# A second bank for h and a second pair for y after the attention, and the low parts of k on VectorE

## The chip, the cores and the metric

The kernel runs on one core of a Trainium2 chip. The metric is the device time of one execution in microseconds (us). The core has five engines, each with a queue of its own that it works through in order: TensorE (PE; its weight loads are a row of their own, PEld), VectorE (DVE), ScalarE (ACT), GpSimd (POOL) and SyncE (SP), which here issues nearly all DMAs. Engines wait for each other by semaphores. Matmuls write to PSUM, which has eight banks of 2 KB per partition; everything else lies in SBUF or DRAM.

## The reference

Three layers, one after the other, all in float32 outside the chip:

```
attn_out: q, k, v of shape (4, 8, 576, 64)
scores = q @ k.T / sqrt(64); scores under (row maximum - tau) are masked out
attn   = exp(scores - max) / (sum + 1e-9);  attn_out = attn @ v
x = attn_out as (2304, 512)
h = x @ w_in (512 x 2048);  g = h * sigmoid(h);  y = g @ w_out (2048 x 512)
a = y @ w_a; b = y @ w_b (512 x 1536 each);  out = (a * b) @ w_o2 (1536 x 512)
```

## The kernel before

**Attention.** A pair of heads of one batch is worked on together. It has nine tiles of 128 query rows against 576 keys, 144 tiles in all. PE writes the scores of a tile to `sa` (two PSUM banks, one buffer; the first 16 tiles also use `sb`); DVE takes the row minimum of the negated scores and moves them to `t` (`L489`), which frees `sa`; ACT takes the exponential (`L503`); DVE masks by the threshold and sums (`L506`); PE turns the masked tile by transposes into `tp` (`L538`, two banks), ACT copies it out, PE multiplies with v (`L583`, bank `av`). The sums are inverted, sent through DRAM (`r_d`, read back as `xi`) and multiplied on by POOL (`L618`); the result goes to DRAM as `xT_d`.

From tile 54 on, heads come in by `split_head`: ACT copies q and k to rounded high parts in the tile `sp` (`L399`), and two POOL instructions, both released by that copy, subtract these to get the low parts: `L405` for q (64 partitions) and `L402` for k (128 partitions, 576 columns). PE then needs two matmuls instead of one slower one (`L473`).

**First MLP.** Nine tiles of 256 tokens by 16 blocks of 128 hidden columns make 144 units, numbered n; a tile j has units 16j to 16j + 15. Weights and activations are each held as a high and a low part. A unit's up-projection is 12 matmuls of 256 columns into the one bank `hb` (`L699`); then ACT takes tanh (`L708`), DVE multiplies the gate out of tanh and h (`L711`), which frees `hb`, ACT rounds it to gh (`L714`) and DVE subtracts for gl (`L717`). The down-projection is 12 more matmuls (`L746`), eight with gh and four with gl, that add to the four outputs of the tile, in the pair of banks `sb`. PE's order is up-projection of unit n, down-projection of unit n - 1, and so on. After a tile's last unit, ACT halves one bank of `sb` (`L763`) and DVE the other (`L765`), which frees the pair, and the result goes to DRAM as `yT_d`. PE works on these units between the attention's instructions and alone after them.

**Second MLP.** Four tiles of 512 tokens and one of 256, by 12 blocks, make 60 units: `ps_a` and `ps_b` (12 matmuls each, `L825`), a copy, a product, high and low part, and 12 matmuls down (`L869`). After the attention its inputs (`yr`, split by `L799` and `L802`) and its weights are made ready: 36 pieces of 512 columns, each some eight instructions on ACT, DVE and POOL (`L312` to `L340`, tiles `wraw`, `wt`, `wc`, `w`).

**PSUM.** During the attention the banks are `sb` 2, `hb` 1, `sa` 2, `tp` 2, `av` 1. After it, `close_attention` gives the last five to `ps_a` and `ps_b`, two each, with one left over. After the first MLP, `close_mlp1` gives `sb` and `hb` to the outputs of the second.

**The order.** Nothing is ordered by hand. `Plan` collects tasks, each with an engine, an estimated cost (`act_ns`, `dve_ns`, `pool_ns`, `pe_ns`), a rank, the tasks it waits for, and the rings (buffers) it takes; it then plays time forward and gives each free engine its ready task of lowest rank. What comes out is the order of each engine's queue in the built program. DVE and POOL are assumed to share a port: a task marked `port` is made longer by what it overlaps with the other engine, at most by its own cost. `closed` and `closed1` are tasks without an instruction, at which pools are closed and opened.

Of the kernel before, what the change touches and what calls it, by code (L numbers as in the profile page):

```python
# [52 lines left out]

WARM = 9

FILL = 0.6
# [148 lines left out]
def fused_kernel(ctx: ExitStack, tc: tile.TileContext, qk, qk2, v, tau, w_in, w_out, w_a, w_b, w_o2, out):  # L205
# [19 lines left out]
    def pool(stack, name, bufs, side="left", **kw):  # L225
# [4 lines left out]
    p1, att = ExitStack(), ExitStack()  # L230
    RINGS = dict(qk=2, sp=2, v=1, t=2, e=4, pa=1, pb=1, sa=1, sb=1, tp=2, hb=1, av=1, x=1, xi=1, rs=1,
                 xr=2, xb=8, g=2, th=1, yo=2, wraw=2, wc=1, wt=2, w=32, w2=4,
# [157 lines left out]
    def split_head(n, b, h):  # L390
        s = {"split": True}

        def load():
            s["r"] = ap["qk"].tile([P, 2 * S], F32, name="qk")
            nc.sync.dma_start(out=s["r"], in_=qk2[b, h])

        def hi():
            s["t"] = pools["sp"].tile([P, 3, S], F32R, name="sp")
            nc.scalar.copy(out=s["t"][:, :2], in_=s["r"].rearrange("p (a s) -> p a s", a=2))  # L399

        def lo_k():
            nc.gpsimd.tensor_tensor(out=s["t"][:, 2], in0=s["r"][:, S:], in1=s["t"][:, 1].bitcast(F32), op=ALU.subtract)  # L402

        def lo_q():
            nc.gpsimd.tensor_tensor(out=s["t"][D:, 0], in0=s["r"][D:, :S], in1=s["t"][D:, 0].bitcast(F32), op=ALU.subtract)  # L405

        ld = dma(n + R_LD, P * 8 * S, load, take=["qk"])
        up = add("ACT", act_ns(2 * S), n + R_SPLIT, hi, [ld], ["sp"], behind=closed0)
        q, k = (add("Pool", pool_ns(S), n + R_SPLIT, f, [up]) for f in (lo_q, lo_k))
        att_tasks.append(ld)  # L410
        pl.free("qk", q, k)
        s["ready"] = [q, k]
        return s
# [273 lines left out]
    def mlp1_up(n, j, f):  # L687

        s = gs[j, f] = {}

        def up(c):
            def fn():
                if c == 0:
                    s["h"] = ps_1.tile([P, 512], F32, name="hb")[:, :TB]
                w = wt["in", c, f // 4]
                o = (f % 4) * P
                x = xs[j]
                for k, (a, xx) in enumerate(((1, x["h", c]), (0, x["h", c]), (0, x["l", c]))):
                    nc.tensor.matmul(s["h"], lhsT=w[:, a, o:o + P], rhs=xx,  # L699
                                     start=(c == 0 and k == 0), stop=(c == NC - 1 and k == 2))  # L700
            return fn
# [18 lines left out]
        for c in range(NC):  # L720
            p = pl.add("PE", 3 * pe_ns(TB), R, up(c),
                       [*x_ready[j, c], *w_ready["in", c, f // 4]], ["hb"] if c == 0 else [], behind=[up_last[0]])
            up_last[0] = p
            w_last["in", c, f // 4] = p
            if f == NF - 1:
                pl.free("xb", p)
        th = pl.add("ACT", act_ns(TB, True), R_AUX, tanh, [p], ["g", "th"])
        ga = pl.add("DVE", dve_ns(TB), R_AUX, gate, [th])
        pl.free("hb", ga)
        hh = pl.add("ACT", act_ns(TB), R_AUX, hi, [ga])  # L730
# [4 lines left out]
    def mlp1_down(n, j, f):  # L735

        prods = [(e, a, "gh") for e in range(NC) for a in (1, 0)] + [(e, 0, "gl") for e in range(NC)]

        def down(k0):
            def fn():  # L740
                if f == 0 and k0 == 0:
                    ys[j] = ps_1.tile([P, 2, 512], F32, name="sb").rearrange("p k (e t) -> p (k e) t", e=2)
                w = wt["out", f]
# [8 lines left out]
        for k0 in (0, 4, 8):  # L752
            p = pl.add("PE", 4 * pe_ns(TB), R, down(k0), [g_ready[j, f][k0 == 8], *w_ready["out", f]],
                       ["sb"] if f == 0 and k0 == 0 else [], behind=[down_last[0]])
            down_last[0] = p
        w_last["out", f] = p
        pl.free("g", p)
        if f == NF - 1:
# [14 lines left out]
            for k in range(2):  # L773
# [4 lines left out]
                y_dma.append(st)  # L778
            pl.free("sb", *evs)

# [32 lines left out]
    def mlp2_up(n, t0, f):  # L813
# [3 lines left out]
        def up(nm, c):  # L817
            def fn():
                if c == 0:
                    s[nm] = pools["ab"].tile([P, T2], F32, name=f"ps_{nm}")  # L820
                w = wt[nm, c, f // 4]
# [22 lines left out]
        for nm in "ab":  # L844
            for c in range(NC):
                p = pl.add("PE", 3 * pe_ns(tn), 1e5 + 2 * n, up(nm, c), [*y2_ready[t0, c], *w_ready[nm, c, f // 4]],
                           ["z" + nm] if c == 0 else [], behind=[up_last[0]])
                up_last[0] = p
# [56 lines left out]
    for b in range(1, B):  # L905
        for c in range(NC):
            pair(b, c, (0, 1))
    units = [(j, f) for j in range(NB) for f in range(NF)]
    for n, u in enumerate(units):
# [11 lines left out]

    def close_attention():
        att.close()
        right.close()
        open_transit()
        pools["w2"] = pool(ctx, "wpool2", RINGS["w2"], "right")
        pools["y"] = pool(ctx, "yb", 6, "right")
        pools["ab"] = pool(ctx, "ps_ab", 2, "right", space=PSUM)

    def close_mlp1():  # L930
        p1.close()
        pools["z"] = pool(ctx, "z", 2)
        pools["ob"] = pool(ctx, "o", 2)
        pools["o_ps"] = pool(ctx, "ps_o", 1, space=PSUM)

    closed = pl.add("none", 1, 0, close_attention, behind=[*att_tasks, *closed0])
    closed1 = pl.add("none", 1, 0, close_mlp1, behind=[up_last[0], down_last[0], closed, *y_dma])
# [58 lines left out]
```

## Time and profile before

| | |
|---|---|
| time, median of 3 runs | 1202.97 us (1200.87 to 1204.55) |
| profiled execution, its own time | 1202.49 us |
| its span | 1200.7 us |
| PE busy | 1162.6 us (97%) |
| DVE busy | 648.1 us (54%) |
| ACT busy | 544.5 us (45%) |
| POOL busy | 278.9 us (23%) |
| mean granted clock of PE | 0.995 |

The profile is of one execution, whose time is the span and the little that lies around it. The granted clock is a share of TensorE's full 2.4 GHz; the other level is 1.2 GHz, 0.50. The shares of busy time are means over stages that differ: the attention (to about 491 us) loads all engines, the first MLP's remaining units (to about 752 us) mostly PE, and the second MLP PE alone. So they are read stage by stage below. In a timeline row, `[1.46 <-DVE th L711]` means that the engine sat idle for 1.46 us ahead of this instruction, and that what ended it was a DVE instruction of line 711 that wrote or read `th`.

### The profile page before, as it was taken

Reading aid. Unit: us, or ns where it says so; the run is one execution under the profiler, and the core shown is the slowest. Engines: PE = TensorE matmul, PEld = TensorE weight load, DVE = VectorE, ACT = ScalarE, POOL = GpSimd, SP = SyncE. Lnnn points to the kernel's source line nnn. Section 1 sums busy time; section 2 is a strip of 40 time slices with the busy share of each in tenths; the row PEclk is TensorE's granted clock in tenths of the full one; section 3 lists DMA queues with packets and bytes.
Section 4 is the critical chain, followed back from the end, with each engine's and each line's share of the span. In section 5 each row is a group of like instructions: output and inputs, shape, how many; then the busy total and the mean of one; then the engine's idle time right before and its main releaser. Section 6 shows DMA issues by size and latency. Waiting matters only on the chain.

```text
span 1200.7 us, 19670 instructions
## 1 busy us (share of the span) xinstructions
PE 1162.6 (97%) x7675; PEld 998.2 (83%) x7675; DVE 648.1 (54%) x1428; ACT 544.5 (45%) x1071; POOL 278.9 (23%) x232
## 2 busy tenths in 40 slices
PE   8889989999999999989999999999999999999998
PEld 5556667888888888889999999888888888888898
DVE  7989898777777777473233258765311211221121
ACT  7777777666666666443233245443211211211121
POOL 3656554233322322130000024443000000000000
PEclk9989999999999999999999999999999999999999
DMA  5655543222322220351010023432200200000000
GB/s 190 195 176 150 160 152 129 80 85 86 97 72 71 89 89 32 101 166 36 1 37 27 1 66 117 152 123 71 70 1 1 70 1 1 18 36 1 1 36 18
DMA packets 43276, 90.14 MB, mean 75 GB/s; under 512 B 4384, under 2 KB 22448, under 8 KB 43184
## 3 DMA queue, kind: packets, MB, share of 16 engines
q1 hardware_dynamic: 43040, 88.89, 23.0%
q8 instruction: 60, 0.98, 0.4%
q14 instruction: 32, 0.26, 0.1%
q10 hardware_dynamic: 144, 0.00, 0.0%
HBM read 74.65 MB, written 14.23 MB: 74 GB/s over the span
## 4 chain that ended last, share of the span: by engine, by line
PE 76%; DVE 10%; DMA 5%; issue 4%; ACT 4%; POOL 1%; SPq 0%; DVEq 0%; ACTq 0%; POOLq 0%
PE op L869 12%; PE ps_b L825 12%; PE ps_a L825 12%; PE hb L699 12%; PE sb L746 12%; PE av L583 5%; PE tp L538 5%; PE sa L473 4%; DVE e L506 3%; DMA xi<-r_d 2%; DVE t L489 1%; DVE wraw L323 1%; DVE thr L497 1%; DVE wc L328 1%; DVE gl L717 1%
## 5 line engine op out<-in xcount | busy, mean ns | idle before, releaser
L699 PE MATMUL hb<-xh,w 128*128 128x256 f32 x1152 | 225.1, 290 | 6.0 <-DVE th L711 3.9
L699 PEld LDWEIGHTS hb<-xh,w 128*128 128x128 f32 x1152 | 179.3, 192 | 14.2 <-DVE th L711 6.2
L746 PE MATMUL sb<-gh,w 128*128 128x256 f32 x1152 | 169.6, 286 | 2.3 <-DVE yo L765 1.8
L699 PE MATMUL hb<-xl,w 128*128 128x256 f32 x576 | 162.9, 283 | 0.0
L835 DVE TENSOR_TENSOR z<-ps_b,z 128x512 f32<-128x512 f32 (+1 forms) x60 | 38.2, 636 | 230.2 <-PE ps_b L825 230.2
L746 PEld LDWEIGHTS sb<-gh,w 128*128 128x128 f32 x1152 | 150.5, 192 | 6.6 <-DVE yo L765 2.8
L506 DVE SCALAR_TENSOR_TENSOR e<-t,thr,e 128x576 f32<-128x576 f32 x128 | 129.7, 1014 | 21.8 <-ACT e L503 20.8
L825 PE MATMUL ps_a<-yh,w 128*128 128x512 f32 (+1 forms) x480 | 137.0, 370 | 0.0
L825 PE MATMUL ps_b<-yh,w 128*128 128x512 f32 (+1 forms) x480 | 136.6, 369 | 0.0
L869 PE MATMUL op<-w,zh 128*128 128x512 f32 x432 | 134.3, 392 | 0.0
L489 DVE TENSOR_SCALAR_CACHE_REDUCE t<-sa,nscale 128x576 f32<-128x576 f32 x128 | 103.6, 809 | 51.6 <-PE sa L473 49.6
L538 PE MATMUL tp<-ident,e 128*128 128x128 f32 x706 | 106.5, 280 | 13.9 <-DVE e L506 10.0
L711 DVE SCALAR_TENSOR_TENSOR th<-th,hb 128x256 f32<-128x256 f32 x144 | 60.2, 418 | 107.2 <-ACT th L708 106.8
L332 POOL TENSOR_TENSOR wt<-wc,wt 128x512 uint32<-128x512 uint32 x68 | 91.2, 1342 | 109.5 <-DVE wc L328 91.3
L503 ACT ACTIVATE e<-t,min 128x576 f32<-128x576 f32 x128 | 99.6, 780 | 28.2 <-DVE t L489 27.5
L708 ACT ACTIVATE th<-hb 128x256 f32<-128x256 f32 x144 | 55.0, 382 | 122.3 <-PE hb L699 113.2
L699 PEld LDWEIGHTS hb<-xl,w 128*128 128x128 f32 x576 | 110.1, 191 | 0.0
L538 PEld LDWEIGHTS tp<-ident,e 128*128 128x128 f32 x706 | 78.8, 141 | 37.4 <-DVE e L506 16.7
L832 ACT COPY z<-ps_a 128x512 f32<-128x512 f32 (+1 forms) x60 | 32.5, 542 | 162.5 <-PE ps_a L825 162.4
L825 PEld LDWEIGHTS ps_a<-yh,w 128*128 128x128 f32 x480 | 87.5, 188 | 16.7
L825 PEld LDWEIGHTS ps_b<-yh,w 128*128 128x128 f32 x480 | 86.8, 188 | 15.4
L717 DVE TENSOR_TENSOR gl<-th,gh 128x256 fp32r<-128x256 f32 x144 | 76.0, 528 | 36.8 <-ACT gh L714 36.4
(85 smaller groups left out, 1901.9 us busy)
## 6 DMA issues: line engine op xcount, KB each, us to landing
qk<-qk SPq DMA_DIRECT2D x20, 576.0 KB
wraw<-w_in SPq DMA_DIRECT2D x16, 512.0 KB
wraw<-w_out SPq DMA_DIRECT2D x16, 512.0 KB
v<-v SPq DMA_DIRECT2D x20, 320.0 KB
wraw<-w_a SPq DMA_DIRECT2D x12, 512.0 KB
wraw<-w_b SPq DMA_DIRECT2D x12, 512.0 KB
wraw<-w_o SPq DMA_DIRECT2D x12, 512.0 KB
xr<-xT_d SPq DMA_DIRECT2D x36, 128.0 KB
```

What stands on the lines that cost most here:

```text
L332: nc.gpsimd.tensor_tensor(out=s["t"], in0=s["c"].bitcast(U32), in1=s["t"], op=ALU.add)
L489: nc.vector.tensor_scalar(out=s["t"], in0=s["s"][:, :, :NH], scalar1=nscale, scalar2=None, op0=ALU.mult, op1=ALU.min, accum_out=s["min"])
L503: nc.scalar.activation(out=s["e"], in_=s["t"], func=AF.Exp, scale=-1.0, bias=s["min"])
L506: nc.vector.scalar_tensor_tensor(out=s["e"], in0=s["s"][:, :, :NH] if early else s["t"], scalar=s["thr"], in1=s["e"], op0=ALU.is_ge if ear ...
L538: nc.tensor.transpose(t["tp"][:, j * P:(j + 1) * P], e["e"][:, o:o + P], ident)
L583: nc.tensor.matmul(s["av"][h * D:(h + 1) * D, :nq], lhsT=v["v"][:, h, k], rhs=s["p"][:, k, h * nq:(h + 1) * nq], start=(k == 0), stop=(k = ...
L699: nc.tensor.matmul(s["h"], lhsT=w[:, a, o:o + P], rhs=xx, start=(c == 0 and k == 0), stop=(c == NC - 1 and k == 2))
L711: nc.vector.scalar_tensor_tensor(out=s["t"], in0=s["t"], scalar=1.0, in1=s["h"], op0=ALU.add, op1=ALU.mult)
L717: nc.vector.tensor_sub(out=s["gl"], in0=s["t"], in1=s["gh"].bitcast(F32))
L746: nc.tensor.matmul(ys[j][:, e, :], lhsT=w[:, a, e * P:(e + 1) * P], rhs=gs[j, f][g], start=(f == 0 and e % 2 == 0 and a == 1), stop=(f == ...
L825: nc.tensor.matmul(s[nm][:, :tn], lhsT=w[:, a, o:o + P], rhs=yy[:, :tn], start=(c == 0 and k == 0), stop=(c == NC - 1 and k == 2))
L869: nc.tensor.matmul(o_ps[t0, i], lhsT=s[z][:, i * P:(i + 1) * P], rhs=wt["o2", f][:, a, :], start=(f == 0 and k == 0), stop=(f == NF2 - 1 a ...
```

## The change

Three things change.

- From tile j = 4 of the first MLP on (unit 64), odd units put h in a bank of their own, `hc`, and even tiles put y in a pair of their own, `sd`. Both are opened by `close_attention` in the banks of the attention, so an odd unit after 64 comes after `closed`.
- `ps_a` and `ps_b` of the second MLP have one buffer each at first (even units); that of the odd units is opened by `close_mlp1`, and odd units come after `closed1`.
- `lo_k` of `split_head` runs on DVE instead of POOL, 20 times.

```diff
+TWO_H = 64
...
         def lo_k():
-            nc.gpsimd.tensor_tensor(out=s["t"][:, 2], in0=s["r"][:, S:], in1=s["t"][:, 1].bitcast(F32), op=ALU.subtract)
+            nc.vector.tensor_tensor(out=s["t"][:, 2], in0=s["r"][:, S:], in1=s["t"][:, 1].bitcast(F32), op=ALU.subtract)
...
-        q, k = (add("Pool", pool_ns(S), n + R_SPLIT, f, [up]) for f in (lo_q, lo_k))
+        q = add("Pool", pool_ns(S), n + R_SPLIT, lo_q, [up])
+        k = add("DVE", dve_ns(S), n + R_SPLIT, lo_k, [up], port=True)
...
+        bank = "hc" if n >= TWO_H and n % 2 else "hb"
...
-                    s["h"] = ps_1.tile([P, 512], F32, name="hb")[:, :TB]
+                    s["h"] = (pools["hc"] if bank == "hc" else ps_1).tile([P, 512], F32, name=bank)[:, :TB]
...
-                       [*x_ready[j, c], *w_ready["in", c, f // 4]], ["hb"] if c == 0 else [], behind=[up_last[0]])
+                       [*x_ready[j, c], *w_ready["in", c, f // 4]], [bank] if c == 0 else [],
+                       behind=[up_last[0], *([closed] if c == 0 and bank == "hc" else [])])
...
-        pl.free("hb", ga)
+        pl.free(bank, ga)
...
+        ring = "sd" if j * NF >= TWO_H and j % 2 == 0 else "sb"
...
-                    s[nm] = pools["ab"].tile([P, T2], F32, name=f"ps_{nm}")
+                    s[nm] = pools["ab", n % 2].tile([P, T2], F32, name=f"ps_{nm}")
...
-                           ["z" + nm] if c == 0 else [], behind=[up_last[0]])
+                           ["z" + nm] if c == 0 else [], behind=[up_last[0], *([closed1] if n % 2 and c == 0 else [])])
...
     def close_attention():
...
+        pools["hc"] = pool(p1, "ps_hc", 1, space=PSUM)
+        pools["ab", 0] = pool(ctx, "ps_ab", 1, "right", space=PSUM)
...
     def close_mlp1():
...
+        pools["ab", 1] = pool(ctx, "ps_ab2", 1, space=PSUM)
```

The costs that `Plan` knows change with this, and so does the order on every engine from the first split head on. In the changed file the same statements stand two to eight lines further down (`L506` is `L509`, `L711` is `L716`, `L765` is `L773`, `L402` is `L404`).

DVE at a pair of split heads late in the attention (`sp` holds the parts of q and k, `t` and `e` a tile of scores before and after the exponential). Before, the masks and minima of these tiles with the gates of two units:

```order
L506 SCALAR_TENSOR_TENSOR e,sum<-t,thr,e 128x576
L711 SCALAR_TENSOR_TENSOR th<-th,hb 128x256
L497 TENSOR_TENSOR thr<-min,tadd 128x1
L489 TENSOR_SCALAR t,min<-sa,nscale 128x576
L717 TENSOR_TENSOR gl<-th,gh 128x256
L506 SCALAR_TENSOR_TENSOR e,sum<-t,thr,e 128x576
L497 TENSOR_TENSOR thr<-min,tadd 128x1
L489 TENSOR_SCALAR t,min<-sa,nscale 128x576
L711 SCALAR_TENSOR_TENSOR th<-th,hb 128x256
```

The same place now:

```order
L509 SCALAR_TENSOR_TENSOR e,sum<-t,thr,e 128x576
L492 TENSOR_SCALAR t,min<-sa,nscale 128x576
L500 TENSOR_TENSOR thr<-min,tadd 128x1
L404 TENSOR_TENSOR sp<-qk,sp 128x576
L492 TENSOR_SCALAR t,min<-sa,nscale 128x576
L716 SCALAR_TENSOR_TENSOR th<-th,hb 128x256
L509 SCALAR_TENSOR_TENSOR e,sum<-t,thr,e 128x576
L722 TENSOR_TENSOR gl<-th,gh 128x256
L500 TENSOR_TENSOR thr<-min,tadd 128x1
L492 TENSOR_SCALAR t,min<-sa,nscale 128x576
L404 TENSOR_TENSOR sp<-qk,sp 128x576
L716 SCALAR_TENSOR_TENSOR th<-th,hb 128x256
```

The low part of k (`L404`) now stands ahead of the row minimum that follows it (`L492`) at the first head, and ahead of a gate (`L716`) at the second.

DVE after the attention, where the inputs and weights of the second MLP come in (`yl`, `wc` and `wraw` are theirs). Before, around the halving of y of tile 3:

```order
L802 TENSOR_TENSOR yl<-yr,yh 128x512 x2
L711 SCALAR_TENSOR_TENSOR th<-th,hb 128x256
L319 TENSOR_SCALAR wc<-wraw 128x512
L323 TENSOR_SCALAR wraw<-wraw 128x512
L717 TENSOR_TENSOR gl<-th,gh 128x256
L328 SCALAR_TENSOR_TENSOR wc<-wc,wraw 128x512
L711 SCALAR_TENSOR_TENSOR th<-th,hb 128x256
L802 TENSOR_TENSOR yl<-yr,yh 128x512
L717 TENSOR_TENSOR gl<-th,gh 128x256
L319 TENSOR_SCALAR wc<-wraw 128x512
L765 TENSOR_SCALAR yo<-sb 128x512
L323 TENSOR_SCALAR wraw<-wraw 128x512
```

Now, around the same halving:

```order
L716 SCALAR_TENSOR_TENSOR th<-th,hb 128x256
L722 TENSOR_TENSOR gl<-th,gh 128x256
L773 TENSOR_SCALAR yo<-sb 128x512
L810 TENSOR_TENSOR yl<-yr,yh 128x512
L716 SCALAR_TENSOR_TENSOR th<-th,hc 128x256
L810 TENSOR_TENSOR yl<-yr,yh 128x512
L722 TENSOR_TENSOR gl<-th,gh 128x256
L321 TENSOR_SCALAR wc<-wraw 128x512
```

The halving (`L765`, now `L773`) stood behind three subtractions of `yl` and four instructions on the first weights; now it stands ahead of all of them. The gate behind it reads `hc`.

PE where the first MLP ends and the second begins (`sb` or `sd` is the last tile's y, `ps_a` the first unit of the second MLP). Before:

```order
L746 MATMUL sb<-gl,w 128x256 x4
L825 MATMUL ps_a<-yh,w 128x512 x2
L825 MATMUL ps_a<-yl,w 128x512
L825 MATMUL ps_a<-yh,w 128x512 x2
L825 MATMUL ps_a<-yl,w 128x512
L746 MATMUL sb<-gh,w 128x256 x8
L746 MATMUL sb<-gl,w 128x256 x4
L825 MATMUL ps_a<-yh,w 128x512 x2
```

Now:

```order
L754 MATMUL sd<-gl,w 128x256 x4
L833 MATMUL ps_a<-yh,w 128x512 x2
L833 MATMUL ps_a<-yl,w 128x512
L754 MATMUL sd<-gh,w 128x256 x8
L754 MATMUL sd<-gl,w 128x256 x4
L833 MATMUL ps_a<-yh,w 128x512 x2
L833 MATMUL ps_a<-yl,w 128x512
L833 MATMUL ps_a<-yh,w 128x512 x2
```

The last down-projection stood behind two of the four parts of the first `ps_a`; now it stands behind one.

## Rows read from the trace of the kernel before

**Rows 1.** Stretches: us, PE, PEld, DVE, ACT, POOL busy (x), PEclk, DMA, GB/s.

```profile
175.00:480.00 305.00, 298.48 (x2382) 261.69 (x2383) 232.75 (x608) 203.65 (x391) 96.99 (x79) 1.00 0.26 84
480.00:545.00 65.00, 60.42 (x478) 57.78 (x478) 39.31 (x80) 28.95 (x66) 15.96 (x14) 0.97 0.39 123
545.00:720.00 175.00, 174.54 (x1443) 173.31 (x1443) 59.02 (x132) 58.36 (x145) 15.49 (x17) 1.00 0.09 28
720.00:755.00 35.00, 33.64 (x249) 31.47 (x249) 28.08 (x50) 17.98 (x37) 16.23 (x12) 1.00 0.44 137
755.00:1140.00 385.00, 385.00 (x1678) 314.75 (x1677) 118.71 (x180) 89.88 (x151) 39.04 (x29) 1.00 0.12 40
```

**Rows 2.** Timeline of PE just after the attention; start, duration, instruction, idle before.

```profile
507.05 0.50 PE L699 MATMUL hb<-xh,w 128*128 128x256 f32 x2 [1.46 <-DVE th L711]
...
513.39 1.96 PE L746 MATMUL sb<-gh,w 128*128 128x256 f32 x8 [1.76 <-DVE yo L765]
...
516.00 0.63 PE L699 MATMUL hb<-xh,w 128*128 128x256 f32 x2
...
517.86 1.12 PE L746 MATMUL sb<-gh,w 128*128 128x256 f32 x8
...
526.40 0.50 PE L699 MATMUL hb<-xh,w 128*128 128x256 f32 x2 [1.18 <-DVE th L711]
```

**Rows 3.** Two us of that stretch, columns as in Rows 1.

```profile
514.00:516.00 2.00, 2.00 (x11) 2.00 (x10) 1.85 (x4) 0.41 (x1) 0.77 (x2) 0.50 0.80 236
```

**Rows 4.** Timeline of all engines over an undisturbed unit of the first MLP.

```profile
495.36 1.12 PE L746 MATMUL sb<-gh,w 128*128 128x256 f32 x8
495.56 0.38 ACT L708 ACTIVATE th<-hb 128x256 f32<-128x256 f32 x1 [1.60 <-PE hb L699]
495.98 0.42 DVE L711 SCALAR_TENSOR_TENSOR th<-th,hb 128x256 f32<-128x256 f32 x1 [1.55 <-ACT th L708]
...
496.43 0.41 ACT L714 CAST gh<-th 128x256 fp32r<-128x256 f32 x1 [0.49 <-DVE th L711]
...
496.80 0.40 PE L699 MATMUL hb<-xh,w 128*128 128x256 f32 x2
...
498.24 0.64 PE L746 MATMUL sb<-gh,w 128*128 128x256 f32 x4
```

**Rows 5.** Timeline of DVE just after the attention.

```profile
504.84 0.69 DVE L802 TENSOR_TENSOR yl<-yr,yh 128x512 fp32r<-128x512 f32 x1 [1.79 <-ACT yh L799]
...
511.25 1.49 DVE L319 TENSOR_SCALAR wc<-wraw 128x512 f32<-128x512 f32 x1
512.66 0.68 DVE L765 TENSOR_SCALAR yo<-sb 128x512 f32<-128x512 f32 x1
```

**Rows 6.** Timeline of PE before the second MLP.

```profile
719.24 0.50 PE L699 MATMUL hb<-xh,w 128*128 128x256 f32 x2 [0.39 <-DVE th L711]
...
731.79 0.50 PE L699 MATMUL hb<-xh,w 128*128 128x256 f32 x2 [0.64 <-DVE th L711]
...
749.24 1.22 PE L746 MATMUL sb<-gh,w 128*128 128x256 f32 x8 [0.42 <-ACT gh L714]
```

**Rows 7.** Who PE waited for in 175:480; us in total, times, longest.

```profile
PE sa L473 <- DVE t L489: 2.5, 4, 1.2
PE tp L538 <- DVE e L506: 2.4, 5, 0.7
```

**Rows 8.** All instructions of L402: duration ns min/median/max, first and last start.

```profile
L402 POOL TENSOR_TENSOR sp<-qk,sp x20: 1412/1434/1954, 193.9 to 456.7; 128x576 fp32r<-128x576 f32 x20
```

**Rows 9.** The same of L405.

```profile
L405 POOL TENSOR_TENSOR sp<-qk,sp x20: 1419/1427/1801, 192.4 to 455.2; 64x576 fp32r<-64x576 f32 x20
```

**Rows 10.** Timeline of POOL and DVE at a split of heads.

```profile
452.41 1.43 POOL L402 TENSOR_TENSOR sp<-qk,sp 128x576 fp32r<-128x576 f32 x1
...
452.50 1.96 DVE L506 SCALAR_TENSOR_TENSOR e<-t,thr,e 128x576 f32<-128x576 f32 x1
```

**Rows 11.** Timeline of DVE with POOL idle.

```profile
460.03 0.81 DVE L506 SCALAR_TENSOR_TENSOR e<-t,thr,e 128x576 f32<-128x576 f32 x1
```

More of the change, by code (lines that the diff above doesn't have):

```diff
@@ L230, in fused_kernel @@
     p1, att = ExitStack(), ExitStack()
-    RINGS = dict(qk=2, sp=2, v=1, t=2, e=4, pa=1, pb=1, sa=1, sb=1, tp=2, hb=1, av=1, x=1, xi=1, rs=1,
+    RINGS = dict(qk=2, sp=2, v=1, t=2, e=4, pa=1, pb=1, sa=1, sb=1, tp=2, hb=1, hc=1, sd=1, av=1, x=1, xi=1, rs=1,
                  xr=2, xb=8, g=2, th=1, yo=2, wraw=2, wc=1, wt=2, w=32, w2=4,
@@ L741, in fn @@
                 if f == 0 and k0 == 0:
-                    ys[j] = ps_1.tile([P, 2, 512], F32, name="sb").rearrange("p k (e t) -> p (k e) t", e=2)
+                    ys[j] = (pools["hc"] if ring == "sd" else ps_1).tile([P, 2, 512], F32, name=ring).rearrange("p k (e t) -> p (k e) t", e=2)
                 w = wt["out", f]
@@ L753, in mlp1_down @@
             p = pl.add("PE", 4 * pe_ns(TB), R, down(k0), [g_ready[j, f][k0 == 8], *w_ready["out", f]],
-                       ["sb"] if f == 0 and k0 == 0 else [], behind=[down_last[0]])
+                       [ring] if f == 0 and k0 == 0 else [], behind=[down_last[0]])
             down_last[0] = p
@@ L778, in mlp1_down @@
                 y_dma.append(st)
-            pl.free("sb", *evs)
+            pl.free(ring, *evs)
     y2, y2_ready, zs, z_ready, o_ps = {}, {}, {}, {}, {}
@@ L907, in fused_kernel, with close_attention @@
             pair(b, c, (0, 1))
+    def close_attention():
+        att.close()
+        right.close()
+        open_transit()
+        pools["w2"] = pool(ctx, "wpool2", RINGS["w2"], "right")
+        pools["y"] = pool(ctx, "yb", 6, "right")
+        pools["hc"] = pool(p1, "ps_hc", 1, space=PSUM)
+        pools["ab", 0] = pool(ctx, "ps_ab", 1, "right", space=PSUM)
+    closed = pl.add("none", 1, 0, close_attention, behind=[*att_tasks, *closed0])
     units = [(j, f) for j in range(NB) for f in range(NF)]
@@ L920, in fused_kernel @@
             pl.free("w", w_last["out", f])
[L922 to L928, printed above, removed]
     def close_mlp1():
@@ L934, in close_mlp1 @@
         pools["o_ps"] = pool(ctx, "ps_o", 1, space=PSUM)
-    closed = pl.add("none", 1, 0, close_attention, behind=[*att_tasks, *closed0])
+        pools["ab", 1] = pool(ctx, "ps_ab2", 1, space=PSUM)
     closed1 = pl.add("none", 1, 0, close_mlp1, behind=[up_last[0], down_last[0], closed, *y_dma])
```

## The prediction

> **What bounds the kernel now.** I read the stretches of the span first [rows 1]. TensorE (PE) is busy for 298.48 of 305 us in the later attention, for all of 385 us in the second MLP, for 174.54 of 175 us in the quiet middle of the first MLP. What PE loses after 175 us is therefore small and sits in three places: 6.52 us in 175 to 480, 4.58 us in 480 to 545 (just after the attention), 1.36 us in 720 to 755 (ahead of the second MLP). Both kernels issue the same matmuls in the same number; only their order differs, and up to the first split head (about 190 us) the order is the same. So the change can only move PE's idle time and its clock.
>
> The timeline of PE names the losses after the attention [rows 2]: 1.46 and 1.18 us waiting for the gate (`L711`), which frees the one h bank, and 1.76 us waiting for the halving of y (`L765`), which frees the one y pair. After the first and the second of these the granted clock is 0.50 [rows 3], that is 1.2 of 2.4 GHz. A down- and an up-projection then take 517.86 - 513.39 = 4.47 us [rows 2] where an undisturbed unit takes 498.24 - 495.36 = 2.88 us [rows 4]: the clock cost 1.59 us on top of the waits.
>
> **Part 1: a second bank for h, a second pair for y.** In an undisturbed unit [rows 4] the gate ends at 495.98 + 0.42 = 496.40 and the next up-projection begins at 496.80: with one bank 0.40 us are to spare. With two banks the up-projection needs the gate of the unit before the last, and the first that still needs this unit is its down-projection at 498.24, which wants gh, done at 496.43 + 0.41 = 496.84: 1.40 us to spare. So a wait of PE for h shrinks by up to 1.00 us, no more, and then turns into a wait for ScalarE's gh. 1.46 becomes 0.46 and 1.18 becomes 0.18 (2.00 saved). The wait for y goes whole (1.76), since tile 4 writes `sd` while tile 3 is still read from `sb`; the order also puts that halving ahead of the y loads' subtractions now, where before a 1.49 us instruction stood right ahead of it [rows 5]. That makes 3.76 us at best. Against it: these waits come from a pile of work on VectorE (DVE), which a faster PE meets sooner. Its lower bound is nothing saved but the 1.76. I take 3.2, near the upper end, since each wait is worked out from its own row.
>
> What these waits hid: an up-projection started earlier asks for tanh and gate earlier, on queues whose order is fixed; nothing that PE needs stands behind them except gh.
>
> **The clock.** With 0.46 us left of 1.46 + 1.76 I expect no fall there: 1.6 saved. If about half of the waits remain it may still fall, so the bounds are 0 and 1.6.
>
> **Part 2: ahead of the second MLP.** The two waits for h there, 0.39 and 0.64 us [rows 6], lie under 1.00 and should go: 1.03. The last down-projection waits 0.42 us for gh. Before it the order now has one quarter of the first up-projection of the second MLP instead of two, so three matmuls of 385.00 / 1678 = 0.229 us [rows 1], 0.69 us, less stands between. That wait grows by between 0 and 0.69; I take 0.35. Net 0.7 saved (bounds 0.3 and 1.0). Odd units of the second MLP now wait for the end of the first: the first of them starts seven matmul groups (7 x 0.69 = 4.8 us) after the last down-projection, and the halving that frees its banks follows three short VectorE instructions, the halving itself 0.68 us [rows 5]; it is hidden, and would cost at most 1 to 2 us if VectorE were over 4 us late.
>
> **Part 3: k's low parts from GpSimd to VectorE.** Twenty instructions of 1.43 us leave GpSimd [rows 8]; PE never waited for them. On VectorE the trace has no such row. The nearest is the subtraction of y's low part, 0.69 us for 512 columns [rows 5], so 576 columns are 0.78 us: 15.5 us in all if nothing is in the way. But in the new order it stands right behind the copy that also releases GpSimd's q part, 1.43 us [rows 9]. While GpSimd worked, a masking of 0.81 us [rows 11] took 1.96 us [rows 10], and GpSimd's 1.43 was untouched. So the upper end for one of them is 0.78 + 1.43 = 2.2 us, 44 us in all.
>
> The Trainium skill, page "SBUF — State Buffer", section "Who interferes with whom", says that a VectorE instruction with two SBUF inputs and a GpSimd instruction that reads SBUF take one pair of ports as an exclusive lock, and the one that comes later is blocked until the other ends. The trace agrees: 1.96 for 0.81. By this rule the two halves of a split, released together, always collide: the 2.2 us above if GpSimd is first, a late q part if VectorE is.
>
> What goes with it: the maskings that the k part held up, 1.96 - 0.81 = 1.15 us a head. Net per head on VectorE between 0.78 - 1.15 = -0.37 and 2.2 - 1.15 = +1.05 us. VectorE is idle for 72 of 305 us there [rows 1], which takes up most of it. The share that came through to PE before: it waited 2.5 + 2.4 = 4.9 us for VectorE [rows 7], against 20 x 1.15 = 23 us of such hold-ups, about 21%. So PE gets 20 x 0.21 x (-0.37 to +1.05), -1.6 to +4.4 us; the middle is +1.4, which I take. Queued behind each k part are the row minimum of the next tile (which frees the scores' bank for PE), its threshold and its mask; PE's other work there is the first MLP's units, of which the new order runs 2.5 more before the last head ends. That the attention ends later costs nothing by itself: the units are the same.
>
> **Sum.** -3.2 - 1.6 - 0.7 + 1.4 = -4.1 us on the profiled execution's 1202.49, which lies 0.48 us under the median of 1202.97: **1198.4 us**. About 0.3%, 3.6 us, is what a measurement here can tell from no change; against the median that is below 1199.4 or above 1206.6.
>
> **Rivals.**
> *The waits move.* PE runs ahead in the pile-up and waits for gh instead; only the y wait goes, the clock still falls. For it: VectorE and ScalarE, not PE, are full there, and gh hangs on the same queues. Against it: the pile is short (rows 2 show three waits in 20 us). Time: -1.76 - 0.7 + 1.4, so 1201.4. No gain at all from the second banks would be the same case with 1202.
>
> *Slower: the k part on VectorE.* If GpSimd wins each collision, a k part takes 2.2 us; the planner's own figure for it is 667 ns and as much again for sharing, 1.33. All 20 are then 0.87 us later than the order assumes, and if PE pays each in full that is 17 us: 1202.5 + 17.4 - 5.5 = 1214. It decides from (5.5 + 3.6) / 20 = 0.46 us per head that reaches PE. For it: the collision is built in. Against it: the same planner misjudged the maskings by a like amount before, and PE lost only 4.9 us in all to VectorE in this stretch.
>
> The Trainium skill's rule above speaks for this rival: by a lock that GpSimd takes first, every head pays the whole 1.43 us.
>
> *Attention gains too.* If the removed GpSimd work was what made the maskings late, the 4.9 us [rows 7] go and no k part is felt: 1202.5 - 5.5 - 4.9 = 1192.1.
>
> **How the numbers follow.** Forecast 0.58 (own range 1196 to 1200.8), waits move 0.22, slower 0.07, attention gains too 0.13. The range 1193 to 1203 leaves out the slower case and part of the tails. Faster by over 0.3%: about 0.42 of the forecast's 0.58 and the 0.13 of the last case, 0.55. Within 0.3%: the rest of the forecast and the moved waits, 0.38. Slower 0.07.
>
> **What will show it.** In the timeline of PE after the attention no wait over 0.6 us for the gate and none for the halving of y, and a granted clock of 1.00 throughout; a remaining wait names gh. Between 175 us and the attention's end PE idle of 5 to 11 us, the k part on VectorE mostly near 2 us and sometimes 0.8. GpSimd's busy time down by some 29 us. The second MLP stays without idle time. Wrong would be: a clock of 0.50 in that place again, waits of PE for the row minimum over 10 us, or a new wait at the first odd unit of the second MLP.

## The result and the profile after

The changed kernel takes **1191.28 us** (1190.53 to 1193.02, four runs), the kernel before in the same rounds 1203.6: a ratio of 0.9903 [0.9883, 0.9924], 11.7 us faster, about three times what I forecast and outside my range. The profiled execution took 1190.77 us, its span 1189.0. Of all executions below, one of the seven of experiment 2 took 2266.40 us and is left out of its ratio; the others lie within 0.4% of their kernel's median.

The stretches of the span again, columns as in [rows 1]. The attention ends no earlier than before (the last product with v starts at 491.3 us before and at 491.7 after), so what is gained there must be other work that PE gets done beside it:

```profile
175.00:480.00 305.00, 301.74 (x2437) 267.85 (x2436) 234.21 (x632) 203.72 (x394) 73.73 (x59) 1.00 0.26 84
480.00:545.00 65.00, 61.34 (x496) 58.45 (x495) 39.04 (x83) 30.50 (x68) 15.34 (x14) 1.00 0.40 123
545.00:720.00 175.00, 175.00 (x1460) 175.00 (x1460) 64.70 (x141) 61.40 (x150) 21.01 (x21) 1.00 0.12 36
720.00:755.00 35.00, 34.69 (x216) 31.21 (x215) 28.23 (x47) 16.74 (x32) 16.71 (x13) 1.00 0.44 136
755.00:1140.00 385.00, 384.26 (x1695) 314.52 (x1695) 113.58 (x174) 88.60 (x150) 33.80 (x25) 1.00 0.12 37
```

Look at the first row against its counterpart: in the same 305 us PE ran 2437 matmuls where it had run 2382. Fifty-five more, nearly all of them matmuls of the first MLP's units, at the 0.12 us from one start to the next of 256 columns, are 6.6 us of work. That is over half of the whole gain, and it lies in the stretch of the attention, where I had expected a loss. VectorE's busy time there hardly moved (232.75 to 234.21). PE's share of busy time shows only half of it: idle time fell from 6.52 to 3.26 us. PE's timeline behind the attention shows why, and what became of the waits (start, duration, instruction, idle before it):

```profile
508.58 0.40 PE L704 MATMUL hc<-xh,w 128*128 128x256 f32 x2
508.82 0.28 PE L704 MATMUL hc<-xl,w 128*128 128x256 f32 x1
510.77 1.22 PE L754 MATMUL sd<-gh,w 128*128 128x256 f32 x8 [1.68 <-ACT gh L719]
...
515.59 0.74 PE L754 MATMUL sd<-gl,w 128*128 128x256 f32 x4 [0.72 <-DVE gl L722]
...
518.07 1.21 PE L754 MATMUL sd<-gh,w 128*128 128x256 f32 x8 [0.30 <-ACT gh L719]
...
525.55 1.21 PE L754 MATMUL sd<-gh,w 128*128 128x256 f32 x8 [0.63 <-ACT gh L719]
...
730.69 1.22 PE L754 MATMUL sd<-gh,w 128*128 128x256 f32 x8 [0.31 <-ACT gh L719]
...
802.38 0.73 PE L833 MATMUL ps_a<-yh,w 128*128 128x512 f32 x2 [0.30 <-POOL w L342]
...
805.85 0.74 PE L833 MATMUL ps_b<-yh,w 128*128 128x512 f32 x2 [0.45 <-DVE w L342]
```

The matmul at 508.82 is recorded as 0.28 us, but its successors usually start 0.12 us behind. The next one starts 1.95 us later, so 1.83 us were lost, of which 1.68 are printed: the first 0.16 us of a wait behind such a matmul lie under its record. Many short waits add up to much that is not printed as idle. I counted from start to start instead: for each pair of neighbouring instructions the time over their usual spacing (the lower quartile of all such pairs), where it is more than 0.02 us. By this count PE lost 15.8 us ahead of transposes and scores in the attention before (from 192 us, 112 places), and 8.4 us after (66 places). [Rows 7] print 4.9 us of it (6.2 with the waits for ScalarE and GpSimd from 192 us on), and PE's whole idle time in [rows 1] is 6.52.

The waits for the gate and for the halving of y [rows 2] are gone, and the clock of 0.50 [rows 3] with them (1.00 in each row of stretches). In their place stand waits for gh, as Part 1 said, but larger: 1.68 in one place. The clock is that of this one execution. At the end, two short waits for weights are new in the second MLP.

The k part on VectorE (`L404`) and GpSimd's q part (`L407`): duration minimum, median and maximum in ns, first and last start, then one pair of splits from the timeline:

```profile
L404 DVE TENSOR_TENSOR sp<-qk,sp x20: 757/759/2032, 192.4 to 456.6; 128x576 fp32r<-128x576 f32 x20
```

```profile
L407 POOL TENSOR_TENSOR sp<-qk,sp x20: 1414/1977/2023, 192.4 to 456.5; 64x576 fp32r<-64x576 f32 x20
```

```profile
452.70 0.76 DVE L404 TENSOR_TENSOR sp<-qk,sp 128x576 fp32r<-128x576 f32 x1 [0.22 <-ACT sp L401]
452.74 2.02 POOL L407 TENSOR_TENSOR sp<-qk,sp 64x576 fp32r<-64x576 f32 x1 [5.12 <-ACT sp L401]
...
456.54 1.43 POOL L407 TENSOR_TENSOR sp<-qk,sp 64x576 fp32r<-64x576 f32 x1 [1.79 <-ACT sp L401]
456.56 2.03 DVE L404 TENSOR_TENSOR sp<-qk,sp 128x576 fp32r<-128x576 f32 x1
...
457.46 0.69 PE L476 MATMUL sa<-sp 128*128 128x288 f32 x4
```

In the first split of each of the ten pairs VectorE starts 0.04 us ahead: it takes 0.76, and GpSimd's q part pays (2.02 for 1.43 [rows 9]). In the second GpSimd is ahead in six of ten pairs, and VectorE pays, 2.03 in the pair shown. The mean of the twenty is 1.154 us. The last row is the first product that reads the first of these splits: it starts 2.70 us after the late q part is done (452.74 + 2.02 = 454.76). What the maskings got back stands in the groups of VectorE between 175 and 490 us (busy total, mean ns, idle before), of before and of after:

```profile
L506 DVE SCALAR_TENSOR_TENSOR e<-t,thr,e 128x576 f32<-128x576 f32 x97 | 98.4, 1015 | 17.4 <-ACT e L503 16.7 <-DVE sum L435 0.3
```

```profile
L509 DVE SCALAR_TENSOR_TENSOR e<-t,thr,e 128x576 f32<-128x576 f32 x97 | 83.2, 858 | 14.1 <-ACT e L506 12.9
...
L404 DVE TENSOR_TENSOR sp<-qk,sp 128x576 fp32r<-128x576 f32 x20 | 23.1, 1154 | 4.8 <-ACT sp L401 4.5
```

The 97 maskings together take 15.2 us less, the k parts 23.1 us more. The waits of PE between 175 and 480 us (us in total, times, longest), against [rows 7]:

```profile
PE sa L476 <- DVE t L492: 1.9, 4, 0.6
PE tp L541 <- ACT pb L548: 1.3, 2, 1.0
```

The waits for the mask (`e`, 2.4 us) are no longer in the list.

To divide the 11.7 us, I cut both programs at the same matmuls and took their starts from PE's timeline (for the last matmul its end), in us. A minus in the forecast is time saved; its first row is the +1.4 of Part 3 less the 1.0 that Part 1 took off the first wait for the gate:

| from matmul to matmul | before | after | difference | forecast |
|---|---|---|---|---|
| first split head (192 us) to the first up-projection of unit 64 | 314.7 | 306.6 | -8.1 | +0.4 |
| to unit 76 | 40.3 | 39.8 | -0.5 | -3.8 |
| to unit 132 | 162.3 | 161.3 | -1.0 | 0 |
| to the first `ps_a` | 37.6 | 35.1 | -2.5 | -0.7 |
| to the last matmul | 449.6 | 450.1 | +0.5 | 0 |

The first row of before holds the 1.46 us wait of [rows 2], so the stretch of the attention itself gained about 6.6 us. By the attention's end 62 up-projections have begun instead of 59.5, and unit 64 starts at 498.9 us instead of 507.05.

### The profile page after: what moved, and what is told of

The parts are those of the page before. It is cut to its first block, busy times and chain, and to the rows that moved or that the text cites. A ratio compares the mean times of both kernels' runs of the same rounds, so it can differ in the third digit from the quotient of the medians.

```text
span 1189.0 us, 19705 instructions
## 1 busy us (share of the span) xinstructions
PE 1154.5 (97%) x7675; PEld 994.4 (84%) x7675; DVE 646.2 (54%) x1448; ACT 543.9 (46%) x1071; POOL 255.2 (21%) x212
## 4 chain that ended last, share of the span: by engine, by line
PE 65%; DVE 5%; DMA 3%; POOL 2%; issue 2%; ACT 1%; SPq 0%; POOLq 0%; DVEq 0%; ACTq 0%
PE op L877 11%; PE ps_b L833 11%; PE ps_a L833 10%; PE hb L704 8%; PE sb L754 7%; PE sd L754 4%; PE hc L704 4%; PE av L586 3%; PE sa L476 3%; PE tp L541 3%; POOL wt L334 2%; DVE wc L330 1%; DMA wraw<-w_a 1%; DVE wraw L325 1%; DVE wc L321 1%
## 5 line engine op out<-in xcount | busy, mean ns | idle before, releaser
L704 PE MATMUL hb<-xh,w 128*128 128x256 f32 x832 | 164.3, 291 | 3.1 <-DVE th L716 1.4
L704 PEld LDWEIGHTS hb<-xh,w 128*128 128x128 f32 x832 | 128.9, 191 | 9.1 <-issue 4.3
L492 DVE TENSOR_SCALAR_CACHE_REDUCE t<-sa,nscale 128x576 f32<-128x576 f32 x128 | 103.5, 808 | 48.9 <-PE sa L476 47.6
L509 DVE SCALAR_TENSOR_TENSOR e<-t,thr,e 128x576 f32<-128x576 f32 x128 | 114.1, 891 | 16.7 <-ACT e L506 15.3
L704 PE MATMUL hb<-xl,w 128*128 128x256 f32 x416 | 117.5, 283 | 0.0
L754 PE MATMUL sb<-gh,w 128*128 128x256 f32 x768 | 115.9, 286 | 0.0
L506 ACT ACTIVATE e<-t,min 128x576 f32<-128x576 f32 x128 | 99.8, 782 | 25.4 <-DVE t L492 24.7
L754 PEld LDWEIGHTS sb<-gh,w 128*128 128x128 f32 x768 | 101.1, 191 | 3.3 <-issue 2.8
L877 PEld LDWEIGHTS op<-w,zh 128*128 128x128 f32 x432 | 80.3, 188 | 16.9
L846 ACT CAST zh<-z 128x512 fp32r<-128x512 f32 (+1 forms) x60 | 34.6, 577 | 128.3 <-DVE z L843 128.3
L722 DVE TENSOR_TENSOR gl<-th,gh 128x256 fp32r<-128x256 f32 x144 | 72.7, 505 | 33.9 <-ACT gh L719 33.6
L833 PE MATMUL ps_a<-yl,w 128*128 128x512 f32 (+1 forms) x240 | 88.9, 370 | 0.0
```

Of the source, the lines that this page charges most:

```text
L492: nc.vector.tensor_scalar(out=s["t"], in0=s["s"][:, :, :NH], scalar1=nscale, scalar2=None, op0=ALU.mult, op1=ALU.min, accum_out=s["min"])
L506: nc.scalar.activation(out=s["e"], in_=s["t"], func=AF.Exp, scale=-1.0, bias=s["min"])
L509: nc.vector.scalar_tensor_tensor(out=s["e"], in0=s["s"][:, :, :NH] if early else s["t"], scalar=s["thr"], in1=s["e"], op0=ALU.is_ge if ear ...
L704: nc.tensor.matmul(s["h"], lhsT=w[:, a, o:o + P], rhs=xx, start=(c == 0 and k == 0), stop=(c == NC - 1 and k == 2))
L722: nc.vector.tensor_sub(out=s["gl"], in0=s["t"], in1=s["gh"].bitcast(F32))
L754: nc.tensor.matmul(ys[j][:, e, :], lhsT=w[:, a, e * P:(e + 1) * P], rhs=gs[j, f][g], start=(f == 0 and e % 2 == 0 and a == 1), stop=(f == ...
```

## The experiments

The leading theory: the gain of the attention comes from GpSimd, which holds up half as many of VectorE's instructions once the k part is off it. The rivals: the changed order of the program makes it; the second banks make it; any one part fewer on GpSimd makes it, whichever it is. Each kernel was timed in five rounds beside the kernel before (medians 1203.1 to 1203.9). "First stage" and "stretch to unit 76" are the first two rows of the table, taken from each kernel's profiled execution. In `diff` fences and in cut lines, `...` stands for what is left out.

**1. The k part alone**, in the kernel before, in plan and instruction:

```diff
-            nc.gpsimd.tensor_tensor(out=s["t"][:, 2], ...
+            nc.vector.tensor_tensor(out=s["t"][:, 2], ...
...
-        q, k = (add("Pool", pool_ns(S), n + R_SPLIT, f, [up]) for f in (lo_q, lo_k))
+        q = add("Pool", pool_ns(S), n + R_SPLIT, lo_q, [up])
+        k = add("DVE", dve_ns(S), n + R_SPLIT, lo_k, [up], port=True)
```

> Only k's low part on VectorE; h and y keep one bank and one pair. The order on PE is that of the changed kernel to the end of the attention. Theory A (the attention gains because VectorE's masks and minima are no longer held up by GpSimd's k part): the attention's gain of 6.7 us stays, so about 1197 against 1203.6 before. Rival B (the second banks carry the gain, and the attention's gain belongs to them in some way): about 1203.

Measured: 1197.91 us, 0.9951 [0.9934, 0.9967], 5.9 us faster. The edit that I had put at +1.4 us is half of the gain.

**2. The second banks alone**: the changed kernel with the k part back on GpSimd.

```diff
-            nc.vector.tensor_tensor(out=s["t"][:, 2], ...
+            nc.gpsimd.tensor_tensor(out=s["t"][:, 2], ...
...
-        q = add("Pool", pool_ns(S), n + R_SPLIT, lo_q, [up])
-        k = add("DVE", dve_ns(S), n + R_SPLIT, lo_k, [up], port=True)
+        q, k = (add("Pool", pool_ns(S), n + R_SPLIT, f, [up]) for f in (lo_q, lo_k))
```

> Only the second bank for h and the second pair for y; k's low part stays on GpSimd. The order on PE in the attention is that of the kernel before. Theory A: the attention is as before, the stretch after it gains about 5 us: about 1198.5. Rival B: about 1191.3, as the changed kernel.

Measured: 1198.82 us, 0.9958 [0.9939, 0.9976], 5.0 us faster. With experiment 1 that makes 10.9 of the 11.7: the parts add up. My terms without the k part were -5.5. But part of the way was another, as PE's first matmul of unit 64 and two stretches behind it show:

```profile
509.28 0.50 PE L703 MATMUL hb<-xh,w 128*128 128x256 f32 x2 [2.14 <-DVE th L715]
```

```profile
508.00:512.00 4.00, 2.72 (x18) 2.72 (x19) 3.35 (x7) 2.67 (x6) 1.17 (x2) 0.84 0.78 276
512.00:516.00 4.00, 4.00 (x27) 4.00 (x27) 3.89 (x6) 2.71 (x7) 1.76 (x2) 0.73 0.63 196
```

The wait for the gate is there and longer (2.14 for 1.46), and the clock falls behind it. The second bank cannot help here: unit 64 is even and writes `hb`, as unit 63 did, and only unit 65 is the first to use `hc`. What the banks gave lies behind this wait: 37.3 us to unit 76 (40.3 before), 161.3 to unit 132 (162.3) and 35.0 to the first `ps_a` (37.6).

**3. The order before, the k part on VectorE**: the planner still takes it for GpSimd's, only the instruction is on VectorE. PE's order is that of before, matmul for matmul.

```diff
-            nc.gpsimd.tensor_tensor(out=s["t"][:, 2], ...
+            nc.vector.tensor_tensor(out=s["t"][:, 2], ...
```

> The kernel before, with the planner still taking k's low part for a GpSimd task, so that PE, ScalarE and the rest of VectorE keep the order of before; only the 20 instructions are issued on VectorE, at the place where the planner let GpSimd begin them. Theory A: the masks are freed all the same, so most of the attention's gain comes, 4 to 7 us: 1197 to 1199.5. Rival C (the new order, with 2.5 more units of the first MLP ahead of the last head, is what gains): no gain or a loss, 1203 or more.

Measured: 1196.86 us, 0.9941 [0.9924, 0.9959], 7.1 us faster. The k part, the maskings (192 to 492 us) and PE's waits there:

```profile
L402 DVE TENSOR_TENSOR sp<-qk,sp x20: 744/748/1282, 196.2 to 452.8; 128x576 fp32r<-128x576 f32 x20
```

```profile
L506 DVE SCALAR_TENSOR_TENSOR e<-t,thr,e 128x576 f32<-128x576 f32 x93 | 82.5, 887 | 17.0 <-ACT e L503 16.6
```

```profile
PE tp L538 <- DVE e L506: 0.5, 2, 0.3
PE sa L473 <- DVE t L489: 0.4, 2, 0.2
```

The first stage takes 308.4 us (314.7), and from start to start PE loses 7.9 us ahead of transposes and scores where it lost 15.8. The gain needs neither the new order nor the banks. In this order the k part stands further back in VectorE's queue and starts 1.6 to 4.5 us after the copy that releases it, when the q part is done: in 19 of 20 cases it takes 0.75 us.

**4. The new order, the k part on GpSimd**: the changed kernel's plan, and the instruction put back.

```diff
-            nc.vector.tensor_tensor(out=s["t"][:, 2], ...
+            nc.gpsimd.tensor_tensor(out=s["t"][:, 2], ...
```

> The changed kernel with its order on PE, but the 20 instructions issued on GpSimd, where the planner let VectorE begin them. Theory A: the masks are held up again, about 6 us over the changed kernel, 1197 or more. Rival C: the order keeps its gain, 1191 to 1192.5.

Measured: 1197.56 us, 0.9946 [0.9927, 0.9965]. The first stage is back at 309.8 us (306.6), and the maskings are held up again:

```profile
L509 DVE SCALAR_TENSOR_TENSOR e<-t,thr,e 128x576 f32<-128x576 f32 x93 | 89.8, 965 | 14.2 <-ACT e L506 13.2
```

In the profiled execution that is half of the way back; in the medians it is all of it, about the time of experiment 2. The runs scatter from 1193.72 to 1200.64, so how much of the attention's gain is the order's stays open here; experiment 3 says none is needed.

**5. The q part on VectorE too**, so that GpSimd does nothing for a split:

```diff
-            nc.gpsimd.tensor_tensor(out=s["t"][D:, 0], ...
+            nc.vector.tensor_tensor(out=s["t"][D:, 0], ...
...
-        q = add("Pool", pool_ns(S), n + R_SPLIT, lo_q, [up])
+        q = add("DVE", dve_ns(S), n + R_SPLIT, lo_q, [up], port=True)
```

> The changed kernel with q's low part on VectorE as well, so that GpSimd takes no part in splitting heads. Theory A (what costs is a VectorE instruction caught behind a GpSimd one): the k parts fall to 0.76 us each, VectorE gains 15 us of work and loses some 12 us of being held up, PE's waits in the attention stay or shrink by 1 to 2 us: 1189.5 to 1191.5. Rival D (VectorE is near its limit there): every added instruction delays a minimum or a mask, 1194 or more.

Measured: 1190.87 us, 0.9895 [0.988, 0.991], not to be told from the changed kernel. Both parts now take 0.76 us each time, the maskings 0.83; the first stage is 2.7 us shorter (303.9), and the stretch to unit 76 is 0.9 longer. There PE waits longer for gh, and the clock falls although both second buffers are there (0.97 between 492 and 545 us):

```profile
507.32 2.08 PE L754 MATMUL sd<-gh,w 128*128 128x256 f32 x8 [3.77 <-ACT gh L719]
```

**6. One pair for y** in the changed kernel:

```diff
-        ring = "sd" if j * NF >= TWO_H and j % 2 == 0 else "sb"
+        ring = "sb"
```

> The changed kernel with the second bank for h but one pair for y. If the two share the gain by the waits they were meant for: the wait for the halving of y comes back after the attention (up to 1.8 us) and 0.2 us at each tile's end, so 1193 to 1194. If the clock falls again, 1.6 more.

Measured: 1194.96 us, 0.9928 [0.9912, 0.9945], an interval that overlaps the changed kernel's. The runs scatter from 1191.55 to 1197.47, and the profiled one took 1192.41, so how much more than its stages show (1.0 us) the pair is worth stays open. The stage from unit 76 to 132 is back at 162.3 us, that is the 1.0 us of the table; the clock stays at 1.00. The remaining waits between 490 and 760 us again name gh and gl:

```profile
PE sb L754 <- ACT gh L719: 3.0, 5, 1.6
PE sb L754 <- DVE gl L722: 0.9, 2, 0.7
```

The wait for the halving of y did not come back with the one pair; nor is it there in experiments 1 and 3, which have one pair too.

**7. One bank for h** in the changed kernel:

```diff
-        bank = "hc" if n >= TWO_H and n % 2 else "hb"
+        bank = "hb"
```

> The changed kernel with the second pair for y but one bank for h. The waits for the gate come back, after the attention and ahead of the second MLP, about 2 us each place, and with them probably the fall of the clock, 1.6: 1195 to 1197. If the bank for h was worth no more than a wait moved from the gate to gh: 1192.

Measured: 1196.33 us, 0.9939 [0.9927, 0.9951], an interval wholly above the changed kernel's. The clock between 492 and 545 us is 0.97 again, the stretch to unit 76 takes 43.4 us (39.8) and that ahead of the second MLP 37.6 (35.1). PE's waits name the gate:

```profile
PE hb L704 <- DVE th L716: 6.6, 7, 3.3
```

**8. Banks, the old order in the attention, the k part on VectorE**: experiment 2 with this one edit.

```diff
-            nc.gpsimd.tensor_tensor(out=s["t"][:, 2], ...
+            nc.vector.tensor_tensor(out=s["t"][:, 2], ...
```

> The two second buffers, with k's low part issued on VectorE but planned as a GpSimd task, so that the attention keeps the order of before. Theory A: the sum of the two single changes measured so far, -7.0 and -5.0 us: about 1191.5, as the changed kernel. Rival C (the new order adds something of its own): 2 us or more over the changed kernel.

Measured: 1190.62 us, 0.9893 [0.9879, 0.9908], the whole gain without the new order in the attention. Two parts fall out otherwise than in the changed kernel: unit 64 waits for the gate again (1.28 us), and ahead of the second MLP 1.9 us of waits for gh are left, so that this stretch takes 37.1 us (35.1).

**9. Later y loads**: in the changed kernel the waits that remain after the attention meet the first loads of y and their splits. Here the loads of the first two tiles wait for the up-projections of units 84 and 104.

```diff
+LATE = {84: 0, 104: 512}
...
-            ld = dma(-1, P * 4 * tn, load, after=[*need, closed], take=["yr"])
+            ld = dma(-1, P * 4 * tn, load, after=[*need, closed, *([late[t0]] if t0 in late else [])], take=["yr"])
...
+    late = {}
...
+        if n in LATE:
+            late[LATE[n]] = up_last[0]
```

> The changed kernel, with the loads and splits of the second MLP's first two token tiles put off from the attention's end to units 84 and 104 of the first MLP. Theory E (what is left of PE's waits after the attention, about 5 us against twelve undisturbed units, comes from these splits on VectorE and ScalarE together with the first weights): 2 to 4 us less than the changed kernel, 1187.5 to 1189.5. Rival F (the weights' pieces alone fill these engines, or the waits come along to the new place): no change, 1191.

Measured: 1188.99 us, 0.9871 [0.985, 0.9891], 2.3 us under the changed kernel, with intervals that overlap. The stretch shows the gain more clearly: to unit 76 it takes 36.1 us (39.8), where twelve undisturbed units are 34.6, and one wait for gh and one for gl (0.2) are left between 493 and 560 us:

```profile
PE sd L755 <- ACT gh L720: 0.7, 1, 0.7
```

**10. Both**: experiments 5 and 9 in one kernel.

```diff
+LATE = {84: 0, 104: 512}
...
-        q = add("Pool", pool_ns(S), n + R_SPLIT, lo_q, [up])
+        q = add("DVE", dve_ns(S), n + R_SPLIT, lo_q, [up], port=True)
...
```

> The same put-off with both low parts of heads on VectorE. Theory E: about 0.5 us under the former, 1187 to 1189. Rival F: 1190.9, as with both low parts on VectorE alone.

Measured: **1186.67 us** (1185.82 to 1186.92), 0.9855 [0.9836, 0.9874], the best of all and below both kernels. Its stretches up to the attention's end and behind it:

```profile
192.00:492.00 300.00, 299.11 (x2423) 267.49 (x2422) 225.52 (x639) 199.72 (x386) 27.78 (x32) 1.00 0.25 82
492.00:545.00 53.00, 52.23 (x430) 51.49 (x429) 29.09 (x60) 22.17 (x53) 15.34 (x15) 1.00 0.33 107
```

PE is printed as idle for 0.89 and 0.77 us of them. From start to start it still loses 6.6 us ahead of transposes and scores in the attention (74 places).

**11. Later y loads in experiment 8**:

```diff
+LATE = {84: 0, 104: 512}
...
```

> The same put-off with k's low part on VectorE in the attention's order of before. Its waits after the attention were 2 us already, so Theory E gives less here, 1 to 2 us: 1188.5 to 1189.5. Rival F: 1190.6.

Measured: 1189.72 us, 0.9882 [0.9864, 0.9901], as experiment 9 within the intervals, and 0.9 us under experiment 8, which is not clear of noise.

**12. The two parts exchanged**: q on VectorE, k on GpSimd, in plan and instruction. This asks whether one part fewer on GpSimd is enough. In the traces the order of PE, ScalarE, VectorE and GpSimd is that of the changed kernel, place for place, but for the twenty exchanges.

```diff
-            nc.vector.tensor_tensor(out=s["t"][:, 2], ...
+            nc.gpsimd.tensor_tensor(out=s["t"][:, 2], ...
-            nc.gpsimd.tensor_tensor(out=s["t"][D:, 0], ...
+            nc.vector.tensor_tensor(out=s["t"][D:, 0], ...
...
-        q = add("Pool", pool_ns(S), n + R_SPLIT, lo_q, [up])
-        k = add("DVE", dve_ns(S), n + R_SPLIT, lo_k, [up], port=True)
+        q = add("DVE", dve_ns(S), n + R_SPLIT, lo_q, [up], port=True)
+        k = add("Pool", pool_ns(S), n + R_SPLIT, lo_k, [up])
```

> The changed kernel with the two low parts swapped: q's on VectorE, k's on GpSimd. Theory A in its general form (one GpSimd instruction of 1.43 us less per head, whichever it is): as the changed kernel, 1190.5 to 1192. Rival G (it had to be k's part, which came second and fell on the mask): 2 us or more over it, 1193.5 to 1197.

Measured: 1204.64 us, 1.0012 [1.0002, 1.0021]: nothing of the gain is left in the time. The second banks still give what they gave (161.3 us to unit 132, 35.0 to the first `ps_a`), but the first stage takes 318.8 us, 4.1 more than in the kernel before. Rival G had the direction, not the size, and its reason, the mask, is not what the trace shows. One split from the timeline, the twenty q parts (mean ns behind the busy total), and PE's waits between 192 and 492 us:

```profile
251.85 1.42 POOL L404 TENSOR_TENSOR sp<-qk,sp 128x576 fp32r<-128x576 f32 x1 [5.51 <-ACT sp L401]
251.87 2.03 DVE L407 TENSOR_TENSOR sp<-qk,sp 64x576 fp32r<-64x576 f32 x1 [0.23 <-ACT sp L401]
```

```profile
L509 DVE SCALAR_TENSOR_TENSOR e<-t,thr,e 128x576 f32<-128x576 f32 x90 | 76.5, 850 | 12.1 <-ACT e L506 11.1
L407 DVE TENSOR_TENSOR sp<-qk,sp 64x576 fp32r<-64x576 f32 x20 | 34.7, 1736 | 5.4 <-ACT sp L401 5.1
```

```profile
PE sa L476 <- DVE t L492: 7.6, 12, 1.2
PE tp L541 <- ACT pb L548: 2.2, 3, 1.3
```

The maskings are as free as in the changed kernel (850 ns). But here GpSimd starts first, by 0.01 us in nine of the ten first splits and by more in nine of the ten second ones, and VectorE's part pays: 1.736 us in the mean where the k part paid 1.154, so 20 x 0.58 = 11.6 us more on VectorE. The first stage is 12.2 us longer than in the changed kernel. PE does not wait for the parts themselves; its waits name the row minimum (`t`), which stands behind them in VectorE's queue. This is the collision of my slower rival. With the same order everywhere, what differs is which part is on which engine, and with it which of the two starts first; moving the start alone was not tried. One part fewer on GpSimd is not enough.

## Why the prediction was wrong

**The step that failed is Part 3**, the k part at +1.4 us. By itself it brought -5.9 [-7.9, -4.0]; in the changed kernel the attention gained 6.6. The forecast's other terms came to -5.5 and the banks alone measured -5.0, so nearly the whole miss of 7.6 us (11.7 less 4.1) is this term, and the rival "attention gains too" (1192.1) is what happened. Three things were wrong in it.

- *The share.* I took from [rows 7] that PE felt 4.9 of 23 us of hold-ups, 21%. From start to start PE had lost 15.8 us ahead of transposes and scores, whatever the cause. So up to some two thirds of the hold-ups may have come through, not a fifth, and a gain of 6 to 7 us was possible. The low end of -1.6 had been worked out with the same share, and so was no bound. But a larger share alone would have made the middle of my term a larger loss; the sign was wrong by the next point.
- *One for one.* I set a hold-up saved on a masking against a microsecond of the k part. The trace shows the k parts with more time (23.1 us) than the maskings gave back (15.2), VectorE's busy time hardly changed, and PE ahead by 55 matmuls. So it matters which instruction is late. PE's waits for the mask vanish, and it has none for the split parts: in the changed kernel both parts of a head are done 0.3 to 13.8 us before the first product that reads them, so a late k part is not itself missed. That holds in experiment 12 too (0.4 to 13.9 us). What a long part costs there is what stands behind it in VectorE's queue: with 1.736 us in the mean the row minimum comes late, and PE waits 7.6 us for it (1.9 in the changed kernel).
- *Who is held up.* I expected mostly 2 us and sometimes 0.8; the median was 0.76. The Trainium skill, page "SBUF — State Buffer", section "Who interferes with whom", says that the later of the two is blocked. The trace agrees in both directions (2.02 for GpSimd's 1.43, 2.03 for VectorE's 0.76). Which of them is later was for the timeline to say, and in before it could not be read.

**Part 1** was right in that waits for h turn into waits for gh, and too large where I looked for it: 2.8 us of these and 0.9 for gl remain between 490 and 560 us, so the stretch to unit 76 gained 0.5 us (with the 1.46 us ahead of it, 2) instead of 3.8. One of its waits it could not reach. The 1.46 us stand ahead of unit 64, which writes the same bank as unit 63; with the attention's order of before the wait is still there (2.14 in experiment 2, 1.28 in experiment 8). In the changed kernel it is gone because unit 64 comes ahead of the pile of work. PE then meets the pile two units later, and experiment 9 shows what was in it: without the early y loads the stretch takes 36.1 us. Removing the bank again (experiment 7) costs 5.0 us. **The clock** held at 1.00 in the profiled execution, as forecast, but the second buffers do not secure it. Behind the attention it fell once in the profile of before, at 513.6 us, when both waits were over. It fell again without the bank for h (experiment 7, a wait of 3.3 us), and also with all second buffers in experiments 2, 5 and 12, at waits of 2.14, 3.77 and 2.3 us; in experiment 4 it stayed at 1.00 with a wait of 2.15. **The y pair** is not shown to be what removed the wait of 1.76: with one pair (experiment 6) it does not come back, so the order, which puts the halving ahead, is enough. The pair gave 1.0 us between units 76 and 132, which I had at nothing: that stretch takes 162.3 us in every kernel here with one pair and 161.3 in every one with two. No view prints the short waits that this is made of.

**Part 2** gave 2.5 us instead of 0.7. The bank for h is needed for it (37.6 us in experiment 7) but is not enough by itself (37.1 in experiment 8). The last down-projection's wait of 0.42 us, which I had growing, is gone. Against it stands +0.5 us in the second MLP: it starts 12 us earlier and waits for its weights twice, 0.30 and 0.45 us. I had called it free of idle time. The wait at its first odd unit did not come, as said.

Of the signs that I named, PE idle of 5 to 11 us to the attention's end was 3.3 us up to 480, and GpSimd's time fell by 23.3 us in that stretch instead of 29, since its q parts became longer.

## What to carry over

Bound the worth of a hold-up by the spacing of matmul starts, not by the printed waits, which miss the first part of each; with a hundred places that was a factor of over two here (15.8 against 6.2 us). Where work moves between two engines that hold each other up, ask which instruction will be late and who waits for it, and which of the two starts first; VectorE's total says neither. If a gain appears at a collision, exchange the two sides once: here a lead of 0.01 to 0.04 us went with all of it.

## What the hardware showed unasked

Two instructions released by the same copy start 0.01 to 0.04 us apart, and the order repeats: VectorE first by 0.04 us in the first split of all ten pairs with k on it, GpSimd first by 0.01 us in nine of ten with q on it. Counted from the copy's end, it is GpSimd's start that differs: 0.13 us in nine of the first ten, 0.08 in all of the other ten, while VectorE starts after 0.09 us in nine of ten of both. What sets it was not tried.

The blocked side pays nearly the other's whole time, whichever side it is: VectorE's 0.76 became 2.03 (+1.27, for GpSimd's 1.43) and GpSimd's 1.43 became 2.02 (+0.59, for VectorE's 0.76), each some 0.16 us less than the time of the one ahead.
